# A spectral filter with a gated feed-forward on one core: every tile in a buffer of its own number, rows normalised in place, statistics on ScalarE, weight scales at once, a new order

## The chip, the cores and the metric

The kernel runs on one core of one Trainium2 chip. The metric is the device time of one execution in microseconds (us). A core has TensorE (PE, matmuls), VectorE (DVE), ScalarE (ACT), GpSimd (POOL) and SyncE (SP, which here issues most DMAs), each with its own stream of instructions. An instruction waits on semaphores for what it reads and for the buffers that it overwrites.

## The reference

```
xn = layernorm(x)                                  # x: 1 x 2048 x 512, f32
s  = irfft2(rfft2(xn) * (w_r + 1j*w_i), (2048, 512))
gate = relu(xn @ W_gate);  up = xn @ W_up          # 512 x 1376
g  = silu((gate * up) @ W_down)                    # 1376 x 512
out = x + s * g
```

## The kernel before

Rows come in eight chunks c of two tiles of 128 rows, and four blocks of four row tiles for the feed-forward. Each factor of a matmul is split into a high and a low fp16 part, and a product is the sum of three passes (high x high, high x low, low x high). The hidden width of 1376 is eleven tiles f, whose weights come in seven groups g of one or two tiles.

*Rows.* x is loaded (`load_x`, line 332), its mean and variance taken (`stats`, 344, on DVE by BN_STATS or on ACT by a Copy and a Square that add up their outputs), the reciprocal deviation found by three Newton steps in a small tile q (`deviation`, `deviations`, 386 to 431), and xn written to xf (`normalise`, 432). Sums of row tiles (sx) are split and stored in DRAM (S_d) and read back by a transposing DMA (xS); so are the rows themselves (X_d, xT).

*Weights.* Raw gate and up tiles are squared and summed (`squares`), PE adds up over partitions, and `group_scale` (620) makes a power of two per tile and side, in a tile p of the group. `group_split` (635) makes high and low parts of the weights (wgu) with it. Its last step, `rhos` (665), copies the scales to csc, inverts them and writes rho, one for each group. `weight_sums` (673) loads raw tiles (rp) again, scales them by csc and adds them up into wT for products of sums (sa, sb, sc: a scheme with three products of half the width in place of four). `down_scale` (735) takes the greatest md*rho over all hidden tiles and, with PE's rows_md, the scale of the down weights wds (scd).

*Feed-forward.* `product` gives gu on PE, `rectify` r on ACT, `hidden` h on DVE with a low part, `down` the product dn, `gate` the activation g on ACT; the gates of early blocks are stored in DRAM (G_d).

*Spectral filter.* `fold` and `split` prepare xs; `first_stage` is the forward transform along rows (s on PE, t on ACT and DVE), stored in A_d and read back as at with the axes exchanged. In `fft_chunk` each of eight chunks of columns goes through y, xx, z and v on PE, with unmixing between on DVE, POOL and ACT; the result t goes to C_d and comes back as ct. `last_stage` is the inverse transform along rows (s on PE, then zz, ae, ye, sv on ACT and DVE), and `finish` multiplies sv by the gate and adds x (xt).

*Order.* The functions only record steps in a Plan (162). `run` (219) issues them by a table of step numbers, ORDER, so that the program's order on every engine is written out; PLACE gives, by a letter, the engine of each step that has a choice (`either`). Tiles of equal size share a tag, and ROOM says how many buffers the tag has: the tile pool hands them out in turn, so a tile waits for the one that had its buffer. Every instruction is issued by a helper, so that all rows of the profile stand under line 155.

Of the kernel before, what the change touches and what calls it, by code (L numbers as in the profile page):

```python
# [1434 lines left out]
```

## Time and profile before

| | us |
|---|---|
| median of 3 runs | 398.07 (398.06 to 398.36) |
| the profiled execution | 398.29 |
| its span in the trace | 396.5 |
| PE busy | 387.1 |
| DVE busy | 313.6 |
| ACT busy | 260.8 |
| POOL busy | 103.7 |

The span leaves 1.8 us around it. TensorE's granted clock is 0.999 of full speed throughout. Rows of the timeline read: start, duration, engine, line, operation, output<-inputs, count, and in brackets the idle time ahead of it with what ended it. In rows of groups, the busy time and the mean duration in ns stand behind the first bar, idle time and its releaser behind the second. Before its first real matmul PE runs small matmuls that only keep it busy.

### The profile page before, as it was taken

What the parts mean: (1) busy time and instruction counts of PE and PEld (TensorE: products, weight loads), DVE (VectorE), ACT (ScalarE), POOL (GpSimd) and SP (SyncE); (2) the same over time, 40 slices, a digit from 0 to 9 for tenths busy, and PEclk for the clock granted to TensorE, in tenths of its full rate; (3) what the DMA queues carried; (4) which work ended last, traced back from release to release, by engine and by line L of the source; (5) the groups of instructions that cost most, each with busy time, mean ns of one, the idle gap of its engine ahead of it and who ended that gap; (6) DMA issues with size and microseconds to landing.
All of it is one profiled execution on the core that took longest, in us unless ns stands there. A gap on an engine that the chain in (4) does not pass through costs nothing.

```text
span 396.5 us, 8764 instructions
## 1 busy us (share of the span) xinstructions
PE 387.1 (98%) x3404; PEld 251.0 (63%) x3404; DVE 313.6 (79%) x610; ACT 260.8 (66%) x512; POOL 103.7 (26%) x92
## 2 busy tenths in 40 slices
...
DVE  4899999998998987985696888864759642889984
...
GB/s 265 409 383 378 132 135 231 258 108 169 316 230 289 299 171 209 256 158 275 183 194 191 144 85 137 66 174 110 250 55 28 107 176 218 249 112 179 159 214 159
DMA packets 67065, 77.94 MB, mean 197 GB/s; under 512 B 29072, under 2 KB 40944, under 8 KB 67024
## 3 DMA queue, kind: packets, MB, share of 16 engines
...
## 4 chain that ended last, share of the span: by engine, by line
PE 66%; DMA 8%; DVE 3%; ACT 3%; SPq 1%; issue 1%; POOL 0%; DVEq 0%
PE dn L155 26%; PE sb L155 9%; PE gu L155 7%; PE sa L155 6%; PE sc L155 6%; DMA ct<-C_d 5%; PE z L155 3%; PE xx L155 3%; PE y L155 2%; DMA xS<-S_d 2%; PE v L155 2%; PE s L155 2%; DMA A_d<-t 1%; SPq L155 1%; DVE xs L155 1%
## 5 line engine op out<-in xcount | busy, mean ns | idle before, releaser
L155 PEld LDWEIGHTS <-wgu 128*128 128x128 f16 x960 | 92.7, 98 | 55.6 <-issue 3.3
L155 PE MATMUL dn<-wds,h 128*128 128x512 f16 (+2 forms) x528 | 117.6, 372 | 1.0 <-DVE wds L155 0.9
L155 PE MATMUL gu<-xT,wgu 128*128 128x512 f16 (+1 forms) x432 | 90.8, 367 | 1.0 <-ACT r L155 1.0
L155 PEld LDWEIGHTS <-h 128*128 128x128 f16 (+1 forms) x594 | 54.6, 98 | 54.3 <-issue 2.3
L155 PEld LDWEIGHTS <-wT 128*128 128x128 f16 x396 | 38.5, 98 | 7.8 <-issue 2.3
L155 PE MATMUL sb<-xS,wT 128*128 128x256 f16 x264 | 32.4, 273 | 1.5 <-ACT sb L155 1.5
L155 PE MATMUL sa<-xT,wgu 128*128 128x256 f16 x264 | 32.5, 273 | 0.0
L155 ACT ACTIVATE g<-dn,cdi 128x512 f32<-128x512 f32 (+1 forms) x16 | 10.7, 671 | 22.5 <-PE dn L155 22.4
L155 DVE TENSOR_TENSOR h<-gu,r 128x512 f32<-128x512 f32 (+3 forms) x30 | 17.8, 596 | 2.5 <-ACT r L155 1.3
L155 DVE TENSOR_TENSOR t<-v,t 128x1024 f16<-128x1024 f32 x8 | 9.7, 1222 | 10.2 <-ACT t L155 10.2
L155 PE MATMUL gu<-xT,wgt 128*64 128x256 f16 (+1 forms) x144 | 16.9, 309 | 0.0
L155 ACT ACTIVATE r<-gu 128x512 f32<-128x512 f32 (+2 forms) x22 | 12.5, 566 | 6.6 <-PE gu L155 6.6
L155 PE MATMUL sb<-xS,wgu 128*128 128x256 f16 x132 | 16.2, 273 | 0.0
L155 PE MATMUL sc<-xS,wgu 128*128 128x256 f16 x132 | 16.2, 273 | 0.0
L155 PE MATMUL sc<-xT,wT 128*128 128x256 f16 x132 | 16.2, 273 | 0.0
L155 ACT ACTIVATE sq<-sc 128x512 f32<-128x512 f32 x11 | 6.5, 591 | 13.7 <-PE sc L155 8.9
L155 ACT ACTIVATE h<-h 128x512 f16<-128x512 f32 (+1 forms) x22 | 13.4, 619 | 3.1 <-DVE h L155 2.4
L155 DVE TENSOR_TENSOR h<-h,h 128x512 f16<-128x512 f32 (+1 forms) x16 | 14.2, 893 | 0.7 <-ACT h L155 0.7
L155 DVE SCALAR_TENSOR_TENSOR wgu<-raw,p,wgu 128x512 f16<-128x512 f32 x20 | 14.4, 746 | 0.2
L155 POOL TENSOR_TENSOR h<-h,h 128x512 f16<-128x512 f32 (+1 forms) x6 | 7.8, 1301 | 23.9 <-ACT h L155 23.9
L155 DVE TENSOR_TENSOR w<-xsp,w 128x1024 f32<-128x1024 f32 (+1 forms) x12 | 12.0, 999 | 2.5 <-POOL xsp L155 2.2
L155 PEld LDWEIGHTS <-wgt 128*64 128x64 f16 (+1 forms) x144 | 9.6, 106 | 6.8 <-issue 0.7
(231 smaller groups left out, 757.3 us busy)
## 6 DMA issues: line engine op xcount, KB each, us to landing
rw<-in_wl SPq DMA_DIRECT2D x8, 512.0 KB, 6.4
A_d<-t SPq DMA_DIRECT2D x16, 256.0 KB, 3.3
wt<-in_wl SPq DMA_DIRECT2D x8, 512.0 KB, 4.5
at<-A_d SPq DMA_DIRECT2D x8, 512.0 KB, 5.0
C_d<-t SPq DMA_DIRECT2D x16, 256.0 KB, 3.5
ct<-C_d SPq DMA_DIRECT2D x16, 256.0 KB, 8.7
x<-in_x SPq DMA_DIRECT2D x7, 512.0 KB
N_d<-xf SPq DMA_DIRECT2D x6, 512.0 KB, 5.6
```

Source lines behind the costliest of these rows:

```text
L155: return lambda *args, **kw: self.tc.keep_in_program_order(f(*args, **kw))
```

## The change

1. Each tile has a buffer of its own number: a string SLOTS names it, and the pool is asked for the tag with that number and one buffer. The counts in ROOM stay, but for the tag p, which goes. 
2. From chunk 2 on x is loaded straight into xf and normalised there.
3. From chunk 2 on all statistics are ACT's, into a junk tile, with the sums of all chunks of a batch in one tile st; the batches of deviations are chunks (2,3) and (4,5,6,7), before (2,3), (4,5) and (6,7).
4. group_scale writes its scales straight to csc; one step, all_scales, inverts all 22 of them and writes all of rho.
5. ORDER (1632 steps, before 1646) and PLACE are new. Costs, due times and port flags of steps changed as well; with the order written out they do not reach the program.

PE has the same 3404 matmuls in other order. DVE has 563 instructions for 610, POOL two fewer; seven high parts of weights go from ACT to DVE.

```diff
-            self.made[name] = self.tiles[name][1]()
+            self.made[name] = self.tiles[name][1](self.slots.get(name, 0))
...
     def run(self):
+        self.slots = {n: int(s, 36) for n, s in zip(self.tiles, SLOTS)}
...
-    T.tile(name, tag, lambda: pools.get(tag, bpool).tile(shape, dtype, name=name, tag=tag, bufs=T.room[tag]))
+    T.tile(name, tag, lambda slot: pools.get(tag, bpool).tile(shape, dtype, name=name, tag=f"{tag}_{slot}", bufs=1))
...
 def load_x(c):
+    if c > 1:
+        tile_of(f"xf{c}", "k4", [P, 2, D + 2], F32)
+        step("SP", .5, lambda: SP.dma_start(T[f"xf{c}"][:, :, 0:D], x[:, 2 * c:2 * c + 2, :]), writes=[(f"xf{c}", "x")], kb=512, lag=2.2)
+        return
...
 def deviations(cs):
+    for j, c in enumerate(cs):
+        tile_of(f"ju{c}", "k2", [P, D], F32)
...
+        for i in range(2):
+            step("ACT", .71, lambda c=c, i=i, junk=junk, part=part: ACT.activation(junk(), T[f"xf{c}"][:, i, 0:D], AF.Copy, accum_out=part(0, i)),
...
+        for i in range(2):
+            step("ACT", .71, lambda c=c, i=i, junk=junk, part=part: ACT.activation(junk(), T[f"xf{c}"][:, i, 0:D], AF.Square, bias=part(1, i), accum_out=part(2, i)),
...
-    def rhos():
-        for i in range(2):
-            DVE.tensor_copy(csc[:, i, fs[0]:fs[-1] + 1], T[f"p{g}"][:, 0, i:2 * nf:2])
-        inverse_of(T[f"p{g}"][:, :, :2 * nf])
-        DVE.scalar_tensor_tensor(rho[:, fs[0]:fs[-1] + 1], T[f"p{g}"][:, 1, 0:2 * nf:2], 2.0 ** 14,
-                                 T[f"p{g}"][:, 1, 1:2 * nf:2], op0=ALU.mult, op1=ALU.mult)
-    step("DVE", .5, rhos, reads=[f"p{g}"], writes=[("rho", g)] + [("csc", f) for f in fs], lead=25)
+def all_scales():
+    def run():
+        inverse_of(csi, csc)
+        DVE.scalar_tensor_tensor(rho, csi[:, 0], 2.0 ** 14, csi[:, 1], op0=ALU.mult, op1=ALU.mult)
+    step("DVE", .35, run, reads=[f"p{g}" for g in range(len(GROUPS))], writes=["rho"], port=True)
```

Three places of the order. First DVE around the scale of the down weights, before: from the maximum over rows (max_md) to the first scaled low part of the down weights (wds), with h_0_1 and h_0_5 parts of the hidden tiles of block 0 and xs the folded rows.

```order
L155 TENSOR_REDUCE max_md<-rows_md 128x1
L155 TENSOR_SCALAR pd<-max_md 128x1
L155 TENSOR_SCALAR pd<-pd 128x1 x2
L155 TENSOR_SCALAR cdi<-pd 128x1
L155 TENSOR_SCALAR scd<-rho,pd 128x11
L155 SCALAR_TENSOR_TENSOR h_0_1_1065<-gu_1_288,ups,r_1_501 128x256
L155 TENSOR_TENSOR h_0_1_1065<-gu_1_288,r_1_501 128x256
L155 TENSOR_TENSOR h_0_5_854<-h_0_5_812,h_0_5_854 128x512
L155 SCALAR_TENSOR_TENSOR wds<-wds,scd 128x512
```

The same stretch now; sx are sums of row tiles:

```order
L165 TENSOR_REDUCE max_md<-rows_md 128x1
L165 TENSOR_SCALAR pd<-max_md 128x1
L165 TENSOR_SCALAR pd<-pd 128x1 x2
L165 TENSOR_SCALAR cdi<-pd 128x1
L165 TENSOR_SCALAR scd<-rho,pd 128x11
L165 TENSOR_TENSOR h_0_7_883<-h_0_7_864,h_0_7_883 128x512
L165 TENSOR_TENSOR sx_0_912<-xf_443 128x512
L165 TENSOR_TENSOR h_0_10_932<-gu_10_611,r_10_859 64x256 x2
L165 TENSOR_TENSOR h_0_10_932<-gu_10_611,r_10_859 32x512
L165 TENSOR_TENSOR sx_1_937<-xf_193,sx_0_912 128x512
L165 SCALAR_TENSOR_TENSOR wds<-wds,scd 128x512
```

Between the scale scd and wds stand now a low part, two sums of rows and h_0_10 in three pieces, in place of the two halves of h_0_1 and a low part.

Second SP around the bounce through A_d, before. A_d takes the outputs t of the forward transform of chunks 4 to 7, E_d its edge, at is the first load of the result; wt are filter weights, rp raw weights, X_d the rows for a later transposing load.

```order
L155 DMA A_d<-t_5_1888 128x1x1024
L155 DMA E_d<-edge_142 64x2x16
L155 DMA A_d<-t_5_1888 128x1x1024
L155 DMA A_d<-t_6_1974 128x1x1024
L155 DMA A_d<-t_7_1978 128x1x1024 x2
L155 DMA A_d<-t_6_1974 128x1x1024
L155 DMA wt_1955<-E_d 2x2x128
L155 DMA wt_2116<-in_wl 128x1024
L155 DMA X_d_78<-x_6_2030 128x2048
L155 DMA at_2146<-A_d 128x2x1024
L155 DMA at_2166<-A_d 128x2x1024
```

Now:

```order
L165 DMA_TRANSPOSE xS_2040<-S_d_0_84 128x16x128
L165 DMA E_d<-edge_143 64x2x16
L165 DMA rp_1_1865<-in_wu 128x4x128
L165 DMA A_d<-t_6_1973 128x1x1024
L165 DMA A_d<-t_7_2003 128x1x1024 x2
L165 DMA A_d<-t_6_1973 128x1x1024
L165 DMA rp_1_1969<-in_wu 128x4x128
L165 DMA X_d_79<-x_7_2068 128x2048
L165 DMA X_d_78<-x_6_2019 128x2048
L165 DMA at_2138<-A_d 128x2x1024
L165 DMA at_2150<-A_d 128x2x1024
```

A transposing load (xS) stands ahead of the last three rows of A_d, a second store to X_d ahead of the loads at, and the loads of filter weights behind them.

Third DVE near the end, before: the low part of hidden tile 4 of the last block (h_3_4_1) and what stands around it. ae, ye and sv belong to the inverse transform, and g_0l to g_3l are gates read back from DRAM.

```order
L155 TENSOR_TENSOR se_4_5123<-se_4_5123,sq_4_5126 128x512
L155 TENSOR_TENSOR ye_4979<-ae_4806,zz_4798 128x4x128
L155 TENSOR_TENSOR sv_5078<-sv_5078,g_0l 128x512
L155 TENSOR_TENSOR sr_4_5156<-sb_4_5014,sr_4_5156 128x512
L155 TENSOR_TENSOR h_3_4_1_5160<-se_4_5123,h_3_4_1_5160 128x512
L155 TENSOR_TENSOR sv_5207<-ye_4979 128x4x128
L155 TENSOR_TENSOR h_3_3_0_5121<-sr_3_4877,h_3_3_0_5121 128x512
L155 TENSOR_TENSOR sv_5202<-ye_5075 128x2x2x127
```

Now:

```order
L165 TENSOR_TENSOR se_4_5033<-se_4_5033,sq_4_5062 128x512
L165 TENSOR_TENSOR h_3_3_1_5057<-se_3_4773,h_3_3_1_5057 128x512
L165 TENSOR_TENSOR ae_5144<-zz_5141 128x4x64
L165 TENSOR_TENSOR sv_5124<-sv_5124,g_0l 128x512
L165 TENSOR_TENSOR xt_0_4838<-xt_0_4838,sv_4791 128x512
L165 TENSOR_TENSOR sv_5124<-sv_5124,g_1l 128x512
L165 TENSOR_TENSOR ye_5147<-ae_5144,zz_5141 128x4x128
L165 TENSOR_TENSOR h_3_4_1_5216<-se_4_5033,h_3_4_1_5216 128x512
L165 TENSOR_TENSOR ye_5147<-ae_5144,zz_5141 128x4x128
```

It is the 522nd of 558 rows before and the 493rd of 519 now: 24 rows of work are left behind it, before 34.

More of the change, by code (lines that the diff above doesn't have):

```diff
@@ L44 @@
 NORMS = ['DVE', 'DVE', 'DVE', 'DVE', 'ACT', 'DVE', 'ACT', 'DVE', 'DVE', 'ACT', 'ACT', 'ACT', 'DVE', 'ACT', 'DVE', 'DVE']
-STATS, ADDS, COPIES = ['DVE', 'DVE', 'ACT', 'DVE', 'ACT', 'ACT', 'ACT', 'ACT'], ['DMA', 'DMA', 'DVE', 'DMA', 'DMA', 'DMA', 'DVE', 'DVE'], [105.83, 202.31, 0.24, 342.73, 748.16, 416.58, 501.03, 895.66]
+ADDS, COPIES = ['DMA', 'DMA', 'DVE', 'DMA', 'DMA', 'DMA', 'DVE', 'DVE'], [105.83, 202.31, 0.24, 342.73, 748.16, 416.58, 501.03, 895.66]
 YCOST, VCOST, SCOST, MODE, JOIN = 0.63, 0.59, 0.6, 0.095, 30.166
@@ L291 @@
     csc = cpool.tile([P, 2, NFT], F32, name="csc")
+    csi = cpool.tile([P, 2, NFT], F32, name="csi")
     sc = cpool.tile([P, NFT], F32, name="scd")
@@ L314, in both, with scale_of, inverse_of @@
         T.either(o if first == "DVE" else o[::-1], reads=reads, writes=writes, **more)
-    def scale_of(sq, out, e):
-        b = out.bitcast(I32)
-        DVE.tensor_scalar(out[:, 0, :], sq, 1e-36, 1e36, op0=ALU.max, op1=ALU.min)
-        DVE.tensor_scalar(b[:, 0, :], b[:, 0, :], 0x7F000000, None, op0=ALU.bitwise_and)
-        DVE.tensor_scalar(b[:, 0, :], b[:, 0, :], -0.5, float((190 + e) << 23), op0=ALU.mult, op1=ALU.add)
-    def inverse_of(out):
-        b = out.bitcast(I32)
-        DVE.tensor_scalar(b[:, 1, :], b[:, 0, :], -1.0, float(254 << 23), op0=ALU.mult, op1=ALU.add)
+    def scale_of(sq, out, e, bits):
+        DVE.tensor_scalar(out, sq, 1e-36, 1e36, op0=ALU.max, op1=ALU.min)
+        DVE.tensor_scalar(bits, bits, 0x7F000000, None, op0=ALU.bitwise_and)
+        DVE.tensor_scalar(bits, bits, -0.5, float((190 + e) << 23), op0=ALU.mult, op1=ALU.add)
+    def inverse_of(to, of):
+        DVE.tensor_scalar(to.bitcast(I32), of.bitcast(I32), -1.0, float(254 << 23), op0=ALU.mult, op1=ALU.add)
     def after_first(name, to):
@@ L351, in stats @@
         tile_of(f"mv{c}", "mv", [P, 2, 2], F32)
-        if STATS[c] == "ACT":
-            tile_of(f"xf{c}", "k4", [P, 2, D + 2], F32)
-            st, mv = (lambda: T[f"st{c}"]), (lambda: T[f"mv{c}"])
-            to = lambda i: T[f"xf{c}"][:, i, 0:D]
-            for i in range(2):
-                step("ACT", .71, lambda i=i: ACT.activation(to(i), T[f"x{c}"][:, i, :], AF.Copy, accum_out=st()[:, i:i + 1]),
-                     reads=x_names(c, i), writes=[(f"st{c}", i), (f"xf{c}", i)])
-            step("DVE", .1, lambda: DVE.tensor_scalar(st()[:, 2:4], st()[:, 0:2], -1.0 / D, None, op0=ALU.mult),
-                 reads=[(f"st{c}", i) for i in range(2)], writes=[(f"st{c}", 2)])
-            step("DVE", .1, lambda: DVE.tensor_scalar(mv()[:, :, 0], st()[:, 0:2], 1.0 / D, None, op0=ALU.mult),
-                 reads=[(f"st{c}", i) for i in range(2)], writes=[(f"mv{c}", 2)])
-            for i in range(2):
-                step("ACT", .71, lambda i=i: ACT.activation(to(i), T[f"x{c}"][:, i, :], AF.Square, bias=st()[:, 2 + i:3 + i], accum_out=st()[:, 4 + i:5 + i]),
-                     reads=[*x_names(c, i), (f"st{c}", 2)], writes=[(f"st{c}", 4 + i), (f"xf{c}", i)])
-            step("DVE", .1, lambda: DVE.tensor_scalar(mv()[:, :, 1], st()[:, 4:6], 1.0 / D, None, op0=ALU.mult),
-                 reads=[(f"st{c}", 4 + i) for i in range(2)], writes=[(f"mv{c}", i) for i in range(2)])
-            return
         if c == 0:
@@ L411, in deviations @@
     def deviations(cs):
-        name = f"q{cs[0]}"
-        tile_of(name, "q4", [P, 3, 4], F32)
+        n, st, q = 2 * len(cs), f"st{cs[0]}", f"q{cs[0]}"
+        tile_of(st, "q", [P, 3, n], F32)
+        tile_of(q, "q4", [P, 3, n], F32)
+        for j, c in enumerate(cs):
+            tile_of(f"ju{c}", "k2", [P, D], F32)
+            junk, part = (lambda c=c: T[f"ju{c}"]), (lambda k, i, w=1, j=j: T[st][:, k, 2 * j + i:2 * j + i + w])
+            for i in range(2):
+                step("ACT", .71, lambda c=c, i=i, junk=junk, part=part: ACT.activation(junk(), T[f"xf{c}"][:, i, 0:D], AF.Copy, accum_out=part(0, i)),
+                     reads=[(f"xf{c}", "x")], writes=[(st, 0, c, i), f"ju{c}"])
+            T.either([("DVE", .1, lambda part=part: DVE.tensor_scalar(part(1, 0, 2), part(0, 0, 2), -1.0 / D, None, op0=ALU.mult), True),
+                      ("ACT", .2, lambda part=part: ACT.activation(part(1, 0, 2), part(0, 0, 2), AF.Copy, scale=-1.0 / D), False)],
+                     reads=[(st, 0, c, i) for i in range(2)], writes=[(st, 1, c)])
+            for i in range(2):
+                step("ACT", .71, lambda c=c, i=i, junk=junk, part=part: ACT.activation(junk(), T[f"xf{c}"][:, i, 0:D], AF.Square, bias=part(1, i), accum_out=part(2, i)),
+                     reads=[(f"xf{c}", "x"), (st, 1, c)], writes=[(st, 2, c, i), f"ju{c}"])
@@ L417, in run @@
         def run():
-            w, y, t = (T[name][:, i, :] for i in range(3))
-            b = T[name].bitcast(I32)
-            for j, c in enumerate(cs):
-                DVE.tensor_scalar(w[:, 2 * j:2 * j + 2], T[f"mv{c}"][:, :, 1], EPS, 64.0 / XS ** 2, op0=ALU.add, op1=ALU.mult)
+            w, y, t = (T[q][:, i, :] for i in range(3))
+            b = T[q].bitcast(I32)
+            DVE.tensor_scalar(w, T[st][:, 2, :], 64.0 / (D * XS ** 2), EPS * 64.0 / XS ** 2, op0=ALU.mult, op1=ALU.add)
             DVE.tensor_scalar(b[:, 1, :], b[:, 0, :], -0.5, float(0x5F3759DF), op0=ALU.mult, op1=ALU.add)
-            for n in range(3):
-                DVE.scalar_tensor_tensor(t, y, -(4.0 ** -n), y, op0=ALU.mult, op1=ALU.mult)
+            for k in range(3):
+                DVE.scalar_tensor_tensor(t, y, -(4.0 ** -k), y, op0=ALU.mult, op1=ALU.mult)
@@ L425, in run @@
                 DVE.tensor_mul(t, t, w)
                 DVE.scalar_tensor_tensor(y, t, 3.0, y, op0=ALU.add, op1=ALU.mult)
-            for j, c in enumerate(cs):
-                at = slice(2 * j, 2 * j + 2)
-                DVE.scalar_tensor_tensor(w[:, at], T[f"mv{c}"][:, :, 0], -1.0, y[:, at], op0=ALU.mult, op1=ALU.mult)
-        step("DVE", DEVIATE[cs[0] // 2 - 1], run, reads=[(f"mv{c}", i) for c in cs for i in range(2 + (STATS[c] == "ACT"))], writes=[(name, 2)], port=True)
+            DVE.tensor_mul(w, T[st][:, 1, :], y)
@@ new lines, in deviations @@
+        step("DVE", 2.3, run, reads=[(st, 2, c, i) for c in cs for i in range(2)], writes=[(q, 2)], port=True)
+        for j, c in enumerate(cs):
+            for i in range(2):
+                k = slice(2 * j + i, 2 * j + i + 1)
+                of = lambda c=c, i=i: T[f"xf{c}"][:, i, 0:D]
+                T.either([("ACT", .62, lambda of=of, k=k: ACT.activation(of(), of(), AF.Identity, bias=T[q][:, 0, k], scale=T[q][:, 1, k]), False),
+                          ("DVE", dve2(512), lambda of=of, k=k: DVE.tensor_scalar(of(), of(), T[st][:, 1, k], T[q][:, 1, k], op0=ALU.add, op1=ALU.mult), True)],
+                         reads=[(f"xf{c}", "x"), (st, 1, c), (q, 2)], writes=[(f"xf{c}", i)])
@@ L439, in normalise @@
                  ("DVE", dve2(512), lambda i=i, to=to, of=of: DVE.tensor_scalar(to(), of(), T[f"mv{c}"][:, i, 0:1], at()[:, i:i + 1], op0=ALU.subtract, op1=ALU.mult), True)]
-            more = dict(reads=[*x_names(c, i), (f"mv{c}", i), (q, 2, i) if c < 2 else (q, 2)] + [(f"mv{c}", 2)] * (STATS[c] == "ACT"),
+            more = dict(reads=[*x_names(c, i), (f"mv{c}", i), (q, 2, i)],
                         writes=[(f"xf{c}", i)])
@@ L620, in group_scale @@
     def group_scale(g):
-        nf = len(GROUPS[g])
+        fs = GROUPS[g]
+        nf = len(fs)
         if g > 2:
@@ L629, in run @@
         def run():
-            scale_of(to()[:, :2 * nf], T[f"p{g}"][:, :, :2 * nf], 9)
+            at = slice(fs[0], fs[-1] + 1)
+            of = lambda t: t.rearrange("p i f -> p f i")[:, at]
+            scale_of(to()[:, :2 * nf].rearrange("p (f i) -> p f i", i=2), of(csc), 9, of(csc.bitcast(I32)))
             if g < HALF:
-                DVE.tensor_scalar(ups[:, g:g + 1], T[f"p{g}"][:, 0, 1:2], 2.0 ** -22, None, op0=ALU.mult)
+                DVE.tensor_scalar(ups[:, g:g + 1], csc[:, 1, g:g + 1], 2.0 ** -22, None, op0=ALU.mult)
         step("DVE", .52 + .07 * (g < HALF), run, reads=[name], writes=[f"p{g}"], port=True)
@@ L639, in group_split @@
             cols = slice(j * P, j * P + fwidth(f))
-            cs = lambda i, j=j: T[f"p{g}"][:, 0, 2 * j + i:2 * j + i + 1]
+            cs = lambda i, f=f: csc[:, i, f:f + 1]
             r = lambda i, cols=cols: T[f"raw{g}_{i}"][:, :, cols]
@@ L663, in group_split @@
                     reads=[f"raw{g}_{i}", f"p{g}", ("wgu", f, 0, i)], writes=[("wgu", f, 1, i)])
-        def rhos():
-            for i in range(2):
-                DVE.tensor_copy(csc[:, i, fs[0]:fs[-1] + 1], T[f"p{g}"][:, 0, i:2 * nf:2])
-            inverse_of(T[f"p{g}"][:, :, :2 * nf])
-            DVE.scalar_tensor_tensor(rho[:, fs[0]:fs[-1] + 1], T[f"p{g}"][:, 1, 0:2 * nf:2], 2.0 ** 14,
-                                     T[f"p{g}"][:, 1, 1:2 * nf:2], op0=ALU.mult, op1=ALU.mult)
-        step("DVE", .5, rhos, reads=[f"p{g}"], writes=[("rho", g)] + [("csc", f) for f in fs], lead=25)
+    def all_scales():
[3 more added lines that the diff above has]
+        step("DVE", .35, run, reads=[f"p{g}" for g in range(len(GROUPS))], writes=["rho"], port=True)
     def weight_sums(n, due):
@@ L687, in weight_sums @@
                 step("ACT", act(512) + .1, lambda part=part, f=f, i=i: ACT.activation(part(), part(), AF.Copy, scale=csc[:, i, f:f + 1]),
-                     reads=[("csc", f)], writes=[(f"{raw}_{i}", j)])
+                     reads=[f"p{g}"], writes=[(f"{raw}_{i}", j)])
         B = lambda i, k: T[f"{raw}_{i}"][:, 2 * k:2 * k + 2]
@@ L743, in tops @@
             DVE.tensor_reduce(md[:, NFT:], md[:, :NFT], axis=AX.X, op=ALU.max)
-        step("DVE", .35, tops, reads=[("md", f) for f in range(NFT)] + [("rho", g) for g in range(len(GROUPS))], writes=["mdt"])
+        step("DVE", .35, tops, reads=[("md", f) for f in range(NFT)] + ["rho"], writes=["mdt"], port=True)
         all_md = greatest("md", md[:, NFT:], ["mdt"], due)
@@ L754, in run @@
             DVE.tensor_scalar(sc, rho, p[:, 1:2], 2.0 ** 13, op0=ALU.mult, op1=ALU.mult)
-        step("DVE", .9, run, reads=["all_md"], writes=["scd"])
+        step("DVE", .9, run, reads=["all_md"], writes=["scd"], port=True)
     def down_weights():
@@ L783, in filter_scale @@
         step("DVE", .15, lambda: DVE.tensor_reduce(mw[:, NCH + 2:NCH + 3], mw[:, :NCH + 2], axis=AX.X, op=ALU.max),
-             reads=[("mw", q) for q in range(NCH + 2)], writes=["mwt"])
+             reads=[("mw", q) for q in range(NCH + 2)], writes=["mwt"], port=True)
         all_mw = greatest("mw", mw[:, NCH + 2:NCH + 3], ["mwt"], due)
@@ L876, in rectify @@
         if c == 0 and f < HALF:
-            for k, by in enumerate((lambda: T[f"p{f}"][:, 0, 0:1], lambda: 2.0 ** -22)):
+            for k, by in enumerate((lambda: csc[:, 0, f:f + 1], lambda: 2.0 ** -22)):
                 at = slice(2 * k, 2 * k + 2)
@@ L1040, in fft_chunk @@
             step("DVE", .3, fill, reads=["spw"], writes=[wtn], port=True)
-            step("DVE", .3, masked, reads=[atn], writes=["am"])
+            step("DVE", .3, masked, reads=[atn], writes=["am"], port=True)
         def y_stage():
@@ L1055, in y_stage @@
                             matmul(y[:, g, t, b, :], at()[rows, b, h, t * P:(t + 1) * P], cm()[rows, b, 0, l, :], start=n == 0, stop=n == 2)
-        step("PE", YCOST, y_stage, mode=2, reads=[atn, f"cm{q}", "cX"] + ["am"] * (q == 0), writes=[f"y{q}"], due=due[0], margin=MARGIN)
+        step("PE", YCOST + .5 * (q == 0), y_stage, mode=2, reads=[atn, f"cm{q}", "cX"] + ["am"] * (q == 0), writes=[f"y{q}"], due=due[0], margin=MARGIN)
         a16 = lambda: T[a16n]
@@ L1067, in corner @@
                     DVE.tensor_scalar(az[:, :, k, :], a16()[:, :, t, 0, 0, 0:64:32], cS[:, 5 + k:6 + k], None, op0=ALU.mult)
-            step("DVE", .3, corner, reads=[(a16n, 0), (a16n, 1)], writes=["az"])
+            step("DVE", .3, corner, reads=[(a16n, 0), (a16n, 1)], writes=["az"], port=True)
         def x_stage():
@@ L1081, in fft_chunk @@
             tile_of("zb", "F", [P, 2, 2], F32)
-        step("PE", pe(12, 256), x_stage, reads=[(a16n, 0), (a16n, 1), "cD"] + ["az"] * (q == 0), writes=[f"xx{q}"] + ["zb"] * (q == 0), due=due[1], margin=MARGIN)
+        step("PE", pe(12, 256) + .1 * (q == 0), x_stage, reads=[(a16n, 0), (a16n, 1), "cD"] + ["az"] * (q == 0), writes=[f"xx{q}"] + ["zb"] * (q == 0), due=due[1], margin=MARGIN)
         xx, xs, xo = (lambda: T[f"xx{q}"]), (lambda: T[xsn]), (lambda: T[f"xo{q}"])
@@ L1168, in v_stage @@
                         matmul(v[64 * b:64 * b + 64, t, :], cm()[at, b, 1, h, :], z16()[at, l, b, :], start=n == 0, stop=n == 2)
-        step("PE", VCOST, v_stage, mode=1, reads=[(z16n, 0), (z16n, 1), f"cm{q}", "cX"], writes=[f"v{q}"], due=due[3], margin=MARGIN)
+        step("PE", VCOST + .42 * (q == 0), v_stage, mode=1, reads=[(z16n, 0), (z16n, 1), f"cm{q}", "cX"], writes=[f"v{q}"], due=due[3], margin=MARGIN)
         t9 = lambda: T[t9n]
@@ L1185, in last_stage @@
             step("SP", .6, lambda i=i: SP.dma_start(T[ctn][64 * i:64 * i + 64].rearrange("s e h d -> s e (h d)"), C_r[2 * c + i]),
-                 reads=[("C_d", q, b) for q in range(NCH) for b in range(2)], writes=[(ctn, i)], lead=14, kb=256)
+                 reads=[("C_d", q, b) for q in range(NCH) for b in range(2)], writes=[(ctn, i)], lead=14, kb=380, lag=4.)
         def run():
```

36 lines of the change are left out of this document (22 added, 14 removed), and 121 rows, old and new, of the table ORDER.

## The prediction, made before the changed kernel ran

> **What bounds the kernel now.** I read the page's busy shares first, then PE's waits, then the timeline at each of those waits, and the chain only for the duration of a matmul.
>
> ```profile
> PE 387.1 (98%) x3404; PEld 251.0 (63%) x3404; DVE 313.6 (79%) x610; ACT 260.8 (66%) x512; POOL 103.7 (26%) x92
> DVE  4899999998998987985696888864759642889984
> ```
>
> PE (TensorE) is busy for 98% of the span at full clock, and both kernels issue the same 3404 matmuls in the same shapes. So the change can only win what PE now waits, and can lose without limit. DVE is nearly full for the first 100 us and again near the end, and there it can hold PE up. PE's waits by releaser:
>
> ```profile
> PE sb L155 <- ACT sb L155: 1.5, 1, 1.5
> ...
> PE gu L155 <- ACT r L155: 1.0, 1, 1.0
> PE dn L155 <- DVE wds L155: 0.9, 1, 0.9
> PE s L155 <- DMA ct<-C_d: 0.4, 1, 0.4
> ```
>
> (The row left out is PE's wait of 1.1 us at the start of the program, which the change does not touch.) Ends of pipelined matmuls are modelled, so I measure each stall from start to start. The timeline of PE gives, for each place, the group ahead of the stall and the one behind it, and the chain gives the pitch of each kind:
>
> ```profile
> 77.83 0.38 PE L155 MATMUL dn<-wds,h 128*128 128x512 f16 x1
> 79.06 0.59 PE L155 MATMUL dn<-wds,h 128*128 128x512 f16 x2 [0.85 <-DVE wds L155]
> ...
> 102.14 0.81 PE L155 MATMUL dn<-wds,h 128*128 128x512 f16 x3
> 103.97 0.81 PE L155 MATMUL gu<-xT,wgu 128*128 128x512 f16 x3 [1.02 <-ACT r L155]
> ...
> 215.83 0.60 PE L155 MATMUL sc<-xS,wgu 128*128 128x256 f16 x4
> 217.92 0.82 PE L155 MATMUL sb<-xS,wT 128*128 128x256 f16 x6 [1.49 <-ACT sb L155]
> ...
> 343.77 0.96 PE L155 MATMUL s<-ct,cR 64*64 64x257 f16 x26
> 345.08 0.85 PE L155 MATMUL s<-ct,cR 64*64 64x257 f16 x22 [0.35 <-DMA ct<-C_d]
> ```
>
> ```profile
> 160.27 7.12 PE dn L155 x33
> 347.35 1.31 PE sc L155 x12
> 348.66 1.44 PE s L155 x48
> ```
>
> A 512-column matmul takes 7.12/33 = 0.216 us, a 256-column one 1.31/12 = 0.109, one of s 1.44/48 = 0.030. Stalls: 79.06 - 77.83 - 0.22 = 1.01; 103.97 - 102.14 - 0.65 = 1.18; 217.92 - 215.83 - 0.44 = 1.65; 345.08 - 343.77 - 0.78 = 0.53. Together **4.4 us**, all there is to win in PE's stream. The profiled execution took 398.29 us, 0.2 above the median of 398.07, so an execution without any stall would be 398.29 - 4.4 = 393.9, or 393.7 beside the median. The tail behind the last matmul stays: ACT's gate, DVE's product, DVE's sum and the store are issued in the same shapes.
>
> ```profile
> 391.99 0.37 ACT L155 ACTIVATE g<-dn_3b,cdi 128x128 f32<-128x128 f32 x1 [1.18 <-PE dn_3b L155]
> ```
>
> **The change part by part.** *Scales and statistics.* On DVE go 14 copies into csc, 6 of 7 rho, 6 of 7 inverses, 2 of 5 row statistics and some tiny rows; 7 high parts of weights come from ACT.
>
> ```profile
> L155 DVE COPY csc<-p 128x2 f32<-128x2 f32 (+1 forms) x14 | 2.5, 222 | 0.0
> L155 DVE SCALAR_TENSOR_TENSOR rho<-p 128x2 f32<-128x2 f32 (+1 forms) x7 | 2.2, 310 | 0.2
> L155 DVE TENSOR_SCALAR p<-p 128x4 int32<-128x4 int32 (+1 forms) x21 | 4.3, 206 | 0.5
> L155 DVE BATCH_NORM_STATS2 st<-x 128x6 f32<-128x512 f32 x5 | 3.4, 679 | 2.8 <-DMA x<-in_x 2.8
> L155 DVE TENSOR_SCALAR wgu<-raw,p 128x512 f16<-128x512 f32 x10 | 4.6, 481 | 0.1
> L155 ACT ACTIVATE wgu<-raw,p 128x512 f16<-128x512 f32 x10 | 6.9, 716 | 0.1
> ```
>
> DVE: 2.5 + 6 x 0.31 + 6 x 0.21 + 2 x 0.68 = 7.0 less, 7 x 0.48 = 3.4 more, so 3.6 us less; the third batch of deviations goes too, some twelve tiny rows. Its price is that rows 4 and 5 now wait for the sums of 6 and 7: their forward transform comes later by the order, just ahead of the bounce below. ACT loses 7 x 0.72 = 5.0 us of these. None of these instructions is one that PE waits for by name in the rows above; all stand in the first 100 us, ahead of rows that are. So they count only through the first two stalls. Two waits are new. The one rho step waits for the last group's scale, which stands 33 rows ahead on DVE: nothing. The deviations of rows 2 and 3 (DVE's q) wait for ACT's sums, where the sums of row 3 were DVE's own: four passes of ACT, 4 x 0.72 = 2.9 us by the row above, against 1.4 on DVE; behind q on DVE queue the low parts of weights and some 45 rows up to the maximum, for which PE waits. ACT has lost 5.0 us ahead of it, so I cost this at nothing, with 0 to 1.5 kept under the start. In-place rows of x and numbered buffers change no duration; they only free tiles at other moments, which the order below already contains. I cost them at nothing; the row nearest to a wait for a buffer is the sb wait of 1.65 us (PE behind ACT's reading of an accumulator), and those accumulators are as many as before. So the ends are -1.65 and +1.65.
>
> *First down product (1.01).*
>
> ```profile
> 69.07 0.28 DVE L155 TENSOR_SCALAR wide_md<-unit,md 128x128 f32<-128x128 f32 x1
> ...
> 77.66 0.68 DVE L155 TENSOR_TENSOR h<-h,h 128x512 f16<-128x512 f32 x1
> 78.26 0.74 DVE L155 SCALAR_TENSOR_TENSOR wds<-wds,scd 128x512 f16<-128x512 f32 x1
> ```
>
> DVE needs 79.00 - 69.35 = 9.65 us from the broadcast maximum to the scaled weight, in an unbroken run, and PE came 1 us too early. In the new order the run from the maximum to that weight holds one row of 1028 columns at 1.1, six of 512 at 0.60, two of 256 at 0.35 and six tiny ones at 0.2: near 6.6 us, against 7.7 us of matmuls between rows_md and that product. This stall goes if DVE reaches the maximum on time; it has 3.6 us less to do up to there. I take 0, with 0 to 1.0 kept. The gu stall behind ACT's r (1.18) lies 25 us later, where ACT too has been relieved; I take 0.2 of it as left, bounds 0 and 1.2.
>
> *The bounce through A_d.* Between the last matmul of the forward row transform and the first y, the new order has 18.9 us of matmuls by the pitches above; the old had 22.2.
>
> ```profile
> 147.38 1.45 PE s L155 x48
> ...
> 171.28 1.99 PE y L155 x105
> ```
>
> ```profile
> 148.21 7.60 SPq L155 DMA_DIRECT2D A_d<-t  x5
> ...
> 159.26 0.34 SPq L155 DMA_DIRECT2D X_d<-x  x1
> 159.78 1.26 SPq L155 DMA_DIRECT2D at<-A_d  x2
> 161.08 5.59 SPq L155 DMA_TRANSPOSE xS<-S_d  x1
> ```
>
> ```profile
> GB/s 265 409 383 378 132 135 231 258 108 169 316 230 289 299 171 209 256 158 275 183 194 191 144 85 137 66 174 110 250 55 28 107 176 218 249 112 179 159 214 159
> ...
> A_d<-t SPq DMA_DIRECT2D x16, 256.0 KB, 3.3
> at<-A_d SPq DMA_DIRECT2D x8, 512.0 KB, 5.0
> ```
>
> The loads at were issued 159.78 - 148.83 = 10.95 us behind that matmul, after the last store (155.8) had landed 3.3 later, and landed 5.0 later: 16.0 us in all, 2.9 less than the new distance. But SP now has a transpose, which holds it 5.59 us in the row above, ahead of the last A_d stores, and a second X_d store ahead of the loads. If the transpose is through before the data of the stores is there it costs nothing; in the worst case all 5.6 are added: a stall of 16.0 + 5.6 - 18.9 = 2.7. I take 0.5, nearer to nothing, because the last store waits for DVE's t until about 7 us behind the matmul anyway, which leaves SP time for the transpose. The Trainium skill, page DMA: Bandwidth & Descriptors, section Queues, rings and completion order, says that each DMA engine takes the descriptors of one queue in ring order, so the second X_d (512 KB) would be moved ahead of the loads; at the highest rate in the GB/s row, 409, that is an estimated 1.3 us more, and the sum would be 0.6 higher. In the trace at landed 5.0 behind its issue with one X_d just ahead, which neither confirms nor denies it.
>
> *The sb stall and the later products* (1.65). Their order is new on PE, DVE and ACT throughout from 175 to 315 us. DVE and ACT are busy 60 to 80% there, and before only one stall arose in 140 us. I take 0.8, half of it, and keep 0 to 2.5. *The loads ct* (0.53): the load that came late now has about 1 us more of matmuls ahead; I take 0.1, bounds 0 and 0.5.
>
> *Start.* PE's head is as dense as before and DVE and ACT have other rows between; before there is no stall from 7.44 to 77 us. I take 0.2, bounds 0 and 1.5 (q, above).
>
> *The end.* By the same pitches PE has 32.5 us of matmuls behind the last inverse row transform s, against 41.6; 9 us of products have gone ahead of it. The last low part of h (h_3_4_1) is first read 12.8 us before PE's end, against 23.7.
>
> ```profile
> 366.58 0.99 DVE L155 TENSOR_TENSOR h<-se,h 128x512 f16<-128x512 f32 x1
> ```
>
> From the last t of the column transform to h_3_4_1 DVE has 63 rows, 37 us by such pitches, where it had 51 and 30 (0.60 us from one row of 512 columns to the next, as 77.66 and 78.26 above show); PE has 56.8 us for them (51.9 before). Behind it stand 24 rows, 13 us, which must be done when the last gate is. Before, that row ended at 367.57, 0.8 us ahead of PE's need at 391.99 - 23.7 = 368.3. Seven more us of DVE work against 4.9 more of PE makes up to 7.0 - 4.9 - 0.8 = 1.3 us late, unless DVE fills gaps that it had around 320 to 337 us, as the earlier products let it. I take 0.8, bounds 0 and 4.
>
> **Sum.** New stalls 0 + 0.2 + 0.5 + 0.8 + 0.1 + 0.2 + 0.8 = 2.6. 398.29 - 4.4 + 2.6 = 396.5 on the profiled execution, less 0.2 is **396.3** beside the median.
>
> **The rivals.** *Traded stalls:* every place is as tight as before, only elsewhere, with the A_d bounce at its worst (2.7) and the products at 1.6: 4.3 for 4.4, time 398.0. For it: a PE at 98% has no slack anywhere, and DVE stays at 9 tenths in its row of slices. Against: less work on DVE and ACT in the first 100 us. *All gone:* 393.8, if every order is punctual; seven places that must all hold. *DVE ends last (slower):* behind the first s PE has 49.4 us left (56.6 before), and DVE some 45 us of rows. Two stretches of 8 us (DVE is the column with x11 and x10) and the group of the last gate products, in the window from 345 us, tell its idle time before:
>
> ```profile
> 336.00:344.00 8.00, 8.00 (x114) 6.79 (x116) 6.35 (x11) 7.08 (x19) 4.17 (x4) 1.00 1.06 219
> 344.00:352.00 8.00, 7.64 (x138) 6.32 (x131) 5.26 (x10) 3.78 (x9) 1.19 (x1) 1.00 0.65 207
> ```
>
> ```profile
> L155 DVE TENSOR_TENSOR sv<-sv,g 128x512 f32<-128x512 f32 x2 | 1.4, 692 | 3.5 <-ACT g L155 3.5
> ```
>
> It idled 1.65 + 2.74 = 4.4 us there for ACT's zz and for PE, and 3.5 in all for the last gates. If all of that recurs, 45 + 4.4 + 3.5 = 53 against 48 us of time is 5 late, and with 1.2 from other places 398.1 - 4.4 + 6.2 = 399.9. It turns into slower from 4 us of lateness on (0.8 us over 398.07 with the 1.2). Against it: the idle around 350 came from products on PE that now stand earlier. *The change does not do what it says* can't be a case of its own: the order shows it.
>
> **How the numbers follow.** A measurement of this kernel can tell about 0.2%, 0.8 us, from no change: faster is below 397.27, slower above 398.87. Forecast (395.0 to 397.2) 0.5; all gone 0.08; traded 0.23; DVE last 0.19. So faster 0.58, same 0.23, slower 0.19. The range goes from all gone, 393.8, to 399.6, within the slow rival, leaving out about 0.15.
>
> **What would show it.** Right: no row of PE's waits on wds or on r near 65 to 105 us; sum of PE's stalls between 2 and 3.5; the largest ones near the y after the last forward transform and in the last 50 us. Wrong in the A_d step: y waiting on at for more than 2.7 or not at all. Wrong at the end: dn waiting for DVE h in the last 20 us by more than 2, or a tail longer than 4.6 us behind the last matmul. If stalls of over 1 us stand in the first 60 us, the start was misjudged: then in-place normalising or the scales hold up what I cost at nothing.

## The result and the profile after

| | before | after |
|---|---|---|
| median, four runs each | 398.22 | 395.37 |
| ratio, 95% interval | | 0.9926 (0.9909 to 0.9943) |
| the profiled execution | 398.29 | 395.73 |
| its span | 396.5 | 393.6 |

The kernel is 2.9 us faster. The forecast was 396.3, 1.8 us faster, with 393.8 to 399.6 as its range. The shares of the engines and DVE's row of slices on the page of the changed kernel:

```profile
PE 386.8 (98%) x3404; PEld 251.1 (64%) x3404; DVE 311.5 (79%) x563; ACT 257.1 (65%) x512; POOL 98.5 (25%) x90
DVE  3899988979787989785899899985658452399995
```

DVE has 2 us less to do in all, yet its row of slices is as full as before, and fuller at the end: the four slices from 344 to 384 us are 9 tenths or more. The waits of PE by releaser:

```profile
PE small L165 <- DVE md L165: 1.1, 1, 1.1
PE rows_mw L165 <- DVE t L165: 0.9, 1, 0.9
PE z L165 <- DVE a L165: 0.2, 1, 0.2
```

None of the four old waits is left (the first row is the start of the program, as before). Of the two new ones the timeline of PE gives the size, from start to start as before:

```profile
160.23 1.46 PE L165 MATMUL dn<-wds,h 128*128 128x512 f16 x6
162.58 0.46 PE L165 MATMUL rows_mw<-wide_mw,ones 128*128 128x128 f32 x2 [0.89 <-DVE t L165]
...
200.56 1.47 PE L165 MATMUL sb<-xS,wT 128*128 128x256 f16 x12
202.22 1.00 PE L165 MATMUL z<-cD,p 128*128 128x128 f16 x15 [0.19 <-DVE a L165]
```

162.58 - 160.23 - 6 x 0.216 = 1.05 us ahead of rows_mw, and 202.22 - 200.56 - 1.31 = 0.35 ahead of a z. So stalls of 4.4 us have become 1.4. The rest of the sum are the two ends of the program:

```profile
7.44 0.60 PE L155 MATMUL head<-unit,xf 128*128 128x128 f32 x4
...
389.95 2.01 PE L155 MATMUL dn_3b<-wds,h 128*128 128x128 f16 x33
```

```profile
7.78 0.60 PE L165 MATMUL head<-unit,xf 128*128 128x128 f32 x4
...
387.79 1.17 PE L165 MATMUL dn_3bb<-wds,h 128*128 128x128 f16 x18
```

PE's first real matmul came 0.34 us later in this execution, and its last ended at 388.96 (before 391.96). From the one to the other PE took 3.3 us less: 3.0 of it are the stalls, and 0.3 lies in smaller differences that were not traced. The span went on for 4.6 us behind the last matmul in both. The spans differ by 2.9, and the execution took 2.1 us around its span for 1.8 before, which leaves the 2.6 by which the two profiled executions differ.

### The profile page after: what moved, and what is told of

The parts are those of the page before. It is cut to its first block, busy times and chain, and to the rows that moved or that the text cites. A ratio compares the mean times of both kernels' runs of the same rounds, so it can differ in the third digit from the quotient of the medians.

```text
span 393.6 us, 8693 instructions
## 1 busy us (share of the span) xinstructions
PE 386.8 (98%) x3404; PEld 251.1 (64%) x3404; DVE 311.5 (79%) x563; ACT 257.1 (65%) x512; POOL 98.5 (25%) x90
## 4 chain that ended last, share of the span: by engine, by line
PE 89%; DVE 6%; ACT 2%; issue 1%; DVEq 0%; ACTq 0%
PE gu L165 27%; PE dn L165 25%; PE sb L165 10%; PE sc L165 7%; PE sa L165 7%; PE z L165 3%; PE s L165 3%; PE small L165 2%; PE xx L165 2%; PE v L165 2%; PE y L165 2%; DVE t L165 1%; DVE a L165 1%; DVE xsp L165 1%; DVE xs L165 1%
## 5 line engine op out<-in xcount | busy, mean ns | idle before, releaser
L165 DVE TENSOR_TENSOR sc<-sb,sk 128x512 f32<-128x512 f32 x11 | 7.7, 698 | 14.5 <-PE sb L165 13.3
L165 POOL DMA_DIRECT2D out<-sv x10 | 8.8, 940 | 31.7 <-DVE sc L165 10.9
L165 POOL TENSOR_TENSOR rp<-rp,rp 128x512 f32<-128x512 f32 x6 | 8.8, 1473 | 23.7 <-ACT xf L165 18.1
L165 DVE SCALAR_TENSOR_TENSOR wgu<-raw,csc,wgu 128x512 f16<-128x512 f32 x20 | 14.5, 745 | 0.1
L165 POOL TENSOR_TENSOR pf<-xsp,w 128x512 f32<-128x512 f32 x5 | 6.8, 1367 | 29.1 <-PE zb L165 17.1
```

Source lines behind the costliest of these rows:

```text
L165: return lambda *args, **kw: self.tc.keep_in_program_order(f(*args, **kw))
```

## The experiments

All runs were compared with the kernel before on the same chip, whose median was 398.0 to 398.2 in each. The medians and ratios:

| run | us | ratio to before |
|---|---|---|
| old, four moves | 398.29 | 1.0010 (0.9998 to 1.0023) |
| old, scales at once | 397.21 | 0.9980 (0.9970 to 0.9991) |
| old, sb and t moved | 397.21 | 0.9977 (0.9964 to 0.9990) |
| old, scales at once and five moves | 397.11 | 0.9970 (0.9955 to 0.9984) |
| new, unchanged, again | 395.69 | 0.9940 (0.9927 to 0.9953) |
| new, scales' work put back | 396.65 | 0.9966 (0.9954 to 0.9978) |
| new, high parts put back | 398.10 | 1.0000 (0.9992 to 1.0009) |
| new, dose in DVE's full stretch | 396.84 | 0.9960 (0.9947 to 0.9973) |
| new, dose in a gap of DVE | 395.31 | 0.9928 (0.9907 to 0.9950) |
| new, rows_mw later | 394.46 | 0.9913 (0.9900 to 0.9925) |
| the same again | 394.91 | 0.9914 (0.9899 to 0.9930) |

**Are four stalls four mends?** The first theory was that PE's stream sets the end and each stall is worth its length, wherever it is removed. Four steps of the old order were moved by a few rows each.

```diff
 # in ORDER: step, and where it went
-  548, 549, 575, 478        # DVE: h_0_1, h_0_1, low part of h_0_5, low part of wds
+  548, 549, 478, 575
-  285, 489, 691             # ACT: xs, wds, r
+  691, 285, 489
-  898, 864, 868, 903        # ACT: h, rp, rp, the copy into sb
+  903, 898, 864, 868
-  1531, 1103                # PE: s, sb
+  1103, 1531
```

> The old kernel with four steps moved by a few rows each, one for each of PE's four stalls (the scaled low part of the down weights ahead of one low part of h on DVE, ACT's r ahead of its xs, ACT's copy into sb ahead of three rows, one s behind one sb on PE). Theory A (PE's stream sets the end, and a stall there is worth its own length): 0.6 + 1.2 + 1.6 + 0.5 = 3.9 of the 4.4 us go, time 398.2 - 3.9 = 394.3. Theory B (what is won at one place is waited for at the next, so that only a new order of everything could win): 397 to 398.2.

398.29, no change: theory A fell. Three of the old stalls are gone from their places, and the first, at wds near 78 us, is down from 1.01 to 0.57 us. Behind the start of the program PE's waits are these now:

```profile
PE gu L155 <- DVE t L155: 1.1, 1, 1.1
PE dn L155 <- DVE wds L155: 1.0, 3, 0.4
PE dn L155 <- ACT g L155: 0.6, 1, 0.6
```

Where PE ran on, it met the next late row: wds three times instead of once, DVE's t in place of ACT's sb, and a gate. For the sb stall the timeline of PE shows it plainly:

```profile
217.77 1.47 PE L155 MATMUL sa<-xT,wgu 128*128 128x256 f16 x12
220.31 4.18 PE L155 MATMUL gu<-xT,wgt 128*128 128x512 f16 x36 [1.07 <-DVE t L155]
```

220.31 - 217.77 - 1.31 = 1.23 us, two matmul groups behind the 1.65 that went. Both waits are in line behind the same rows of ACT.

**Clearing the second wait too.** So ACT's t of that chunk was moved with the copy into sb, and nothing else.

```diff
-  898, 864, 868, 903, 1240  # ACT: h, rp, rp, the copy into sb, t of column chunk 0
+  903, 1240, 898, 864, 868
```

> The old kernel with ACT's copy into sb and ACT's t of the first column chunk both moved ahead of three rows that nobody waits for near 216 us. In the run with four moves the sb stall of 1.65 went and one of 1.23 came 2.4 us later, for DVE's t behind that ACT's t. Theory A (a second wait stood hidden right behind the first, and clearing both wins): the 1.65 go, time 398.0 - 1.5 = 396.5. Theory B (PE's lead is always used up by the next wait): stalls of the same sum elsewhere, 397.7 to 398.2.

397.21: it won 0.9 us (0.4 to 1.4) of the 1.5, between the two theories. The timelines of PE, DVE and ACT show what took back most of the 1.65:

```profile
217.53 1.94 ACT L155 ACTIVATE rp<-rp,csc 128x512 f32<-128x512 f32 x3
219.50 0.69 DVE L155 TENSOR_TENSOR rp<-rp,rp 128x512 f32<-128x512 f32 x1 [1.12 <-ACT rp L155]
222.45 1.55 DVE L155 TENSOR_TENSOR h<-gu,r 64x256 f32<-64x256 f32 x3
224.06 0.88 PE L155 MATMUL y<-cm,at 64*128 64x64 f16 x48 [0.94 <-DVE h L155]
```

The expectation called the three rows ones that nobody waits for. Nobody on PE does; but DVE sat 1.1 us for ACT's rp, and behind that row stood the h for which PE's y waited at 224 us. The price of a moved row was paid through two queues. And the wait for ct is absent here, though nothing near it was moved. Of the loads ct whose landing the traces have, the slowest took 9.5 us from issue to landing here and 10.5 in the profile of the kernel before; why is not shown. So 0.5 of the 4.4 us did not hang on a row beside it.

**Does relief of DVE make room?** The scales alone, in the old order (the new group_scale and the one rho step, in the place of the last of the seven old ones; the other six issue nothing):

```diff
 def rhos():
-    for i in range(2):
-        DVE.tensor_copy(csc[:, i, fs[0]:fs[-1] + 1], T[f"p{g}"][:, 0, i:2 * nf:2])
-    inverse_of(T[f"p{g}"][:, :, :2 * nf])
-    DVE.scalar_tensor_tensor(rho[:, fs[0]:fs[-1] + 1], ...
+    scaled.append(g)
+    if len(scaled) == len(GROUPS):
+        inverse_of(csi, csc)
+        DVE.scalar_tensor_tensor(rho, csi[:, 0], 2.0 ** 14, csi[:, 1], op0=ALU.mult, op1=ALU.mult)
```

> The old kernel and order with the scales alone changed: written straight to csc, one inverse and one rho in place of seven groups of copies, inverses and rho. DVE loses some 4 to 5 us of small rows ahead of 64 us. Theory A (DVE's load ahead of the first down product made that stall): the stall of 1.0 us near 78 us goes, the three others stay, time 397.0 to 397.4. Theory B (the order alone made it): no change, 398.2.

397.21, 0.8 us (0.4 to 1.2) won: the time of theory A, but not by its account alone. PE's waits behind the start:

```profile
PE sb L155 <- ACT sb L155: 1.5, 1, 1.5
PE gu L155 <- ACT r L155: 1.0, 1, 1.0
PE dn L155 <- DVE wds L155: 0.5, 1, 0.5
```

The wait for wds near 78 us fell from 0.9 to 0.5, not to nothing, and the one for ct went, which neither theory had: 0.4 us of the gain is at the first place and 0.5 at the other, so that the time fell into theory A's range is partly luck. Then the same in the other direction, the old work added to the new kernel:

```diff
+            for i in range(2):
+                DVE.tensor_copy(csi[:, i, at], csc[:, i, at])
+            inverse_of(csi[:, :, at], csi[:, :, at])
+            DVE.scalar_tensor_tensor(rho[:, at], csi[:, 0, at], 2.0 ** 14, csi[:, 1, at], op0=ALU.mult, op1=ALU.mult)
```

> The new kernel with the work of the old scales put back on DVE as extra rows behind each group's scale (two copies, an inverse and a rho for each of seven groups, 28 rows, 5 to 6 us ahead of 60 us); they write tiles that the new step writes again. Theory A (this load made the old stall at the first down product): DVE had 1.7 us of slack and 0.8 idle there, so PE stalls by 2 to 3.5 there, time 397 to 399. Theory B (the new order has room for it): 395.4 to 395.8.

396.65, 1.0 to 1.3 above the new kernel (395.69 in its second measurement, 395.37 in its first) and between the ranges of the theories. Neither theory named the place: the first down product still has no wait, and PE waits much earlier, at 27.7 us, for a low part of a weight.

```profile
PE gu L165 <- DVE wgu L165: 0.6, 1, 0.6
```

**Moves and relief together.** Perhaps the moves had failed only for want of slack on DVE. The scales at once, the four moves and the t in the old order:

> The old kernel with the scales taken at once, the four moves and ACT's t moved as well, the rest of the order untouched. Theory A (the moves alone failed because DVE had no slack ahead of 125 us, where the down weights' low parts came late three times, 0.4 to 0.7 us each; the scales give it): stalls of 1 us in all are left of 4.4, time 394.5 to 395.0. Theory B (only a new order of the whole removes them): 396.5 to 397.2, as with the scales alone.

397.11: what the scales give alone (397.21), and theory A fell again. The waits for wds became fewer and shorter; the y that waited in the run with sb and t moved and a gate remain:

```profile
PE y L155 <- DVE h L155: 0.9, 1, 0.9
PE dn L155 <- ACT g L155: 0.6, 1, 0.6
```

**ACT's statistics and DVE's high parts.** The new kernel takes sums on ACT and gives high parts of weights to DVE. The latter alone was undone, by PLACE's letters, with the order as it is.

```diff
+  place = {95: "A", 107: "A", 133: "A", 151: "A", 153: "A", 155: "A", 165: "A", 167: "A", 97: "D", 119: "D"}.get(len(self.steps), place)
```

> The new kernel and order with the high parts of the weights on the engines that had them before (eight back to ACT, two back to DVE), so 6 x 0.72 = 4.3 us more on ACT and 6 x 0.48 = 2.9 less on DVE, all between 20 and 62 us. Theory A (statistics on ACT fit only because DVE took these rows: ACT is busy for 9.0 to 10.0 of every 10 us from 20 to 60 us): PE waits 1 to 4 us there, time 396.4 to 399. Theory B (the two engines share one load, and where a row stands does not matter while DVE wins what ACT loses): 395.1 to 395.7.

398.10: all of the gain is gone, 2.4 us beside the new kernel on the same chip (395.69), in theory A's range. The busy time of the engines by stretches of 10 us, in the new kernel and then in this one (columns PE, PEld, DVE, ACT, POOL, clock, DMA share, GB/s):

```profile
20.00:30.00 10.00, 10.00 (x61) 5.75 (x59) 9.79 (x28) 9.97 (x30) 0.00 (x0) 1.00 0.93 332
30.00:40.00 10.00, 10.00 (x61) 5.44 (x60) 9.48 (x29) 9.90 (x29) 0.00 (x0) 1.00 0.72 234
40.00:50.00 10.00, 10.00 (x65) 5.09 (x62) 9.63 (x26) 8.98 (x19) 0.00 (x0) 1.00 0.94 337
50.00:60.00 10.00, 10.00 (x48) 4.52 (x47) 8.49 (x19) 9.90 (x25) 2.29 (x2) 1.00 0.90 205
```

```profile
20.00:30.00 10.00, 9.43 (x57) 5.33 (x56) 8.71 (x26) 8.30 (x24) 0.00 (x0) 1.00 0.74 263
30.00:40.00 10.00, 9.08 (x53) 4.79 (x52) 8.32 (x24) 9.90 (x31) 0.00 (x0) 1.00 0.90 293
40.00:50.00 10.00, 10.00 (x65) 5.02 (x64) 6.99 (x22) 10.00 (x22) 0.00 (x0) 1.00 0.72 245
50.00:60.00 10.00, 8.97 (x43) 3.97 (x42) 8.66 (x15) 9.90 (x24) 1.10 (x1) 1.00 0.71 195
```

From 40 to 50 us DVE drops from 9.6 to 7.0 us, ACT rises to all ten, and from 20 to 60 us PE loses 2.5 us of busy time, in waits for ACT alone:

```profile
PE gu L165 <- ACT r L165: 1.6, 2, 1.0
PE sum L165 <- ACT wgu L165: 0.9, 1, 0.9
```

These stand at 28.4 and 57.4 us (r) and at 36.3 (sum). The timeline of ACT shows where the first of them comes from:

```profile
21.94 0.72 ACT L165 ACTIVATE wgu<-raw,csc 128x512 f16<-128x512 f32 x1 [1.66 <-DVE csc L165]
```

A high part that went back to ACT stands in its queue ahead of the r, and ACT idled 1.66 us there for DVE's scale. It is ACT's only wait from 18 to 60 us; the other two stalls stand behind a full ACT.

**How tight is the end?** DVE's row for the low part h_3_4_1 was issued three times, with the same values, and in another run a row of DVE in a gap.

```diff
 for n in ORDER:
-    self.steps[n].fn()
+    for k in range(3 if n == 1120 else 1):     # 1088 in the other run
+        self.steps[n].fn()
```

> The new kernel with DVE's row for the low part h_3_4_1 issued three times in place of once (the same values each time), so 1.2 us more of DVE ahead of the product that reads it. Theory A (DVE's order in the last 50 us fits PE's by a margin of 0.5 us: the row ended at 375.65 and is first read at 388.96 - 12.84 = 376.1): PE waits 0.7 for DVE's h there, time 395.4 + 0.7 = 396.1. Theory B (DVE has room there): 395.4.

> The same dose of 1.2 us in a gap of DVE: its row for sc of chunk pair 3 near 339.1 us issued three times, behind which DVE idles 1.2 us. Both theories: no change, 395.4 (up to 395.6). If the time rises by 0.5 or more, what counts is DVE's sum of work from there to the end and not its place.

In the full stretch the dose cost 1.1 to 1.5 us (396.84), more than theory A's 0.7; in the gap nothing (395.31). The timelines of DVE and PE in the first:

```profile
375.04 2.13 DVE L165 TENSOR_TENSOR h<-se,h 128x512 f16<-128x512 f32 x3
377.23 0.40 PE L165 MATMUL dn_3b<-wds,h 128*128 128x128 f16 x4 [0.99 <-DVE h L165]
```

The stall is 1.15 by its distance from the matmul ahead, which started at 376.02. The three rows took 2.13 us where one took 0.68 in the new kernel, so the dose was 1.45 and not 1.2, and some 0.3 of the margin of 0.5 was there. At this row of the new kernel DVE is ahead of PE by less than half a us.

**The stall that is left.** rows_mw is a small matmul. The timeline of DVE in the new kernel shows its operand and what it waited for:

```profile
156.95 0.28 DVE L165 TENSOR_SCALAR wide_mw<-unit,mw 128x128 f32<-128x128 f32 x1
160.15 2.48 DVE L165 TENSOR_TENSOR t<-s,t 128x896 f16<-128x896 f32 x4 [1.72 <-ACT t L165]
```

The operand wide_mw was ready at 157.2 us, but by SLOTS rows_mw stands in the accumulator that held the forward transform's s of chunk 6, and DVE's t reads that until 162.4 (the third of its four rows). The row that reads its result stands far behind on DVE. It was moved behind six products.

```diff
-  507, 776, 777, 778, 779, 780, 781     # PE: rows_mw, six products dn of block 1
+  776, 777, 778, 779, 780, 781, 507
```

> The new kernel with PE's rows_mw, before which PE waits 1.05 us for DVE's t near 162.6 us, moved behind six more down products. Theory A (PE's stream alone sets the end): 395.4 - 1.05 = 394.3. Theory B (DVE, busy without a gap from 345 to 384 us, sets the end by now): at most half of it, 394.9 to 395.4, and PE waits for DVE's h in the last 20 us.

> The new kernel with rows_mw behind six more down products, again, for its gain over the new kernel on one chip. PE's stall of 1.05 us is its whole gain: 394.3 to 394.5, against 395.4. If the first run's gain was chance: 395.4.

394.46 and 394.91, ratios of 0.9913 and 0.9914, against 0.9926 and 0.9940 of the new kernel: on the chip that ran both, 0.8 us faster (395.69 to 394.91). Theory A holds: one wait of 0.2 us is left to PE behind the start of the program, and PE has no wait for DVE's h in the last 20 us, which theory B expected. This version beats both kernels.

```profile
PE z L166 <- DVE a L166: 0.2, 1, 0.2
```

Not tried: the new order without numbered buffers (by the order, 88 of its 591 tiles are still read when a pool that hands out buffers in turn would have given theirs to the next tile, so it can't run that way with as many buffers), rows in place alone, and the larger batch of deviations alone.

## Why the prediction was right, and where its sum was off

The bound and the direction held: the stream of PE sets the end, 4.4 us was all to win, and the new order wins most of it. The steps:

*The first two stalls* (1.0 and 1.18; 0 and 0.2 forecast): both are gone. The reason given was DVE's 3.6 us less of small rows; over the whole program DVE's busy time fell by 2.1. The runs bear the reason out in part: scales at once win 0.8 in the old order and cost 1.0 when put back in the new, but not at the place that I named. In the new kernel the first down product has DVE's row ready in good time, at 68.2 for PE's 69.7 (the timelines of DVE and of PE below); with the old work put back it is the weights' stretch from 20 to 30 us that stalls.

```profile
67.47 0.74 DVE L165 SCALAR_TENSOR_TENSOR wds<-wds,scd 128x512 f16<-128x512 f32 x1
```

```profile
69.73 0.82 PE L165 MATMUL dn<-wds,h 128*128 128x512 f16 x3
```

*High parts to DVE* were costed as 3.4 us of DVE work set against 5.0 of ACT, with no effect of their own. By the rows of the traces they are six and not seven (ten on each engine before; four on ACT and sixteen on DVE now), so 2.9 against 4.3. The effect was missed: undone in this order it costs 2.4 us, as much as the whole gain on that chip. The forecast had the relief of ACT as cover for the new wait on its sums (0 to 1.5) and asked only what the cover was worth at one place. Two things act in that run, and it does not part them: from 30 to 60 us ACT is full, but ahead of PE's stall at 28.4 it had idled 1.66 us for DVE's scale (8.30 us busy for 9.97 from 20 to 30), because a returned row stands at a place in the order that was made for DVE.

*Numbered buffers* were costed at nothing, and as rows of their own they are. But with buffers handed out in turn this order can't be had (88 tiles), so whatever the order wins is theirs as well.

*The bounce through A_d* (0.5 forecast, up to 2.7): nothing. The timeline of SP's queue in the new kernel, DVE's copy am, which is the first to read the first load at, and y on PE:

```profile
156.92 2.55 SPq L165 DMA_TRANSPOSE xS<-S_d  x1
162.50 3.18 SPq L165 DMA_DIRECT2D A_d<-t  x4
166.97 1.63 SPq L165 DMA_DIRECT2D X_d<-x  x2
169.10 1.81 SPq L165 DMA_DIRECT2D at<-A_d  x2
```

```profile
175.91 0.20 DVE L165 COPY am<-at 128x126 f16<-128x126 f16 x1 [1.32 <-DMA at<-A_d]
```

```profile
178.51 0.23 PE L165 MATMUL y<-cm,at 64*128 64x64 f16 x4
```

And the loads' time from issue to landing, of the rows on tile at whose landing the trace has:

```profile
DMA to landing us min/median/max: 4.3/4.7/5.2
```

The transpose held SP for 2.55 us, not 5.6, and was through before the last stores had their data. The first load at was issued at 169.10, and DVE sat idle for it until 175.91: 6.8 us, and 2.6 ahead of y. So the 4.3 to 5.2 of the view are those of later loads at, issued from 227 us on, with no store to X_d just ahead. In all eight runs of the new order the first load took 6.2 to 6.9 us by the same reading. The 5.0 that the prediction gave to the old first load is the time of another one too, the only load at whose landing the old trace has. The Trainium skill, page DMA: Bandwidth & Descriptors, section Queues, rings and completion order, says that each DMA engine takes the descriptors of one queue in ring order, from which the prediction estimated 1.3 us more; the trace agrees, with 6.8 for at most 5.2. That the two stores are the cause is not shown, since no run takes them away. The forecast had room for it: PE's distance from the last forward matmul to y was 20.2 us (158.3 to 178.5), for the most part the 18.9 counted and the stall of 1.05 at rows_mw.

*The later products and sb* (0.8 forecast): 0.35 at z. The largest stall, 1.05 at rows_mw, stands ahead of them, at a place that the prediction did not have; there PE waited for one of the accumulators that it named as unchanged in number, only for another tile.

*The end* (0.8 forecast, up to 4): nothing in the new kernel, but the mechanism was right: of a dose of 1.45 us, 1.15 came through. The reckoning of 1.3 us late took 7 us more of DVE's work up to h_3_4_1. From the last t of the column transform to the end of that row DVE is busy for 37.5 us, before 32.5, so 5.0 more, and that alone turns 1.3 late into 0.7 early; the row ended at 375.65, 0.5 ahead of its first use. That DVE would fill its gaps, the way out that the prediction named, is not what happened: slices 31 to 35 of its row, from 295 to 344 us now, read 8 4 5 2 3, where they read 9 6 4 2 8 before. The work is done in the unbroken run behind 344 us.

So new stalls of 2.6 were forecast and 1.4 came. By the prediction's own signs the first two stalls were judged rightly (no wait on wds or r), the sum was not (1.4, below its 2 to 3.5), nor was the bounce (y not waiting at all), and neither of the two places that it named for the largest stalls has one. That the total came within a us is in part luck: the terms for the start, the bounce, ct and the end came to nothing, and the 1.05 at rows_mw was in no term. What the prediction did not see is how little the old order could be mended in place: the rival that stalls are traded was right for the four moves, and wrong for a new order of the whole.
